# A linear-attention and feed-forward kernel: rows of x and w_in in a new order, a planner that counts TensorE's modes, and new order tables

## The chip, the cores and the metric

The kernel runs on one core of one Trainium2 chip. The metric is device time in microseconds (us) of one execution; lower is better. Engine names in the profile are PE (TensorE's matmuls), PEld (TensorE's loads of stationary operands, which overlap the matmuls), DVE (VectorE), ACT (ScalarE), POOL (GpSimd) and SP (SyncE, which here only issues transfers).

## What is computed

The reference has two parts. The first is a linear attention with a decaying state, for 4 batches of 8 heads, 768 positions and 48 values per head (inputs r, k, v, w and u):

```python
for t in range(S):
    cur = np.einsum('bhd,bhe->bhde', u[None] * kt, vt)
    y[:, :, t] = np.einsum('bhd,bhde->bhe', rt, state + cur)
    state = wt[:, :, :, None] * state + np.einsum('bhd,bhe->bhde', kt, vt)
```

Its output, put together over the heads, is x with 3072 rows of 384 values. The second part is `h = maximum(x @ w_in, 0)` and then `(h * h) @ w_out`, with w_in 384 x 2048 and w_out 2048 x 384, both in 64-bit floats in memory.

## The kernel before

The 768 positions are cut into 6 chunks of 128. An attention unit is one chunk of one batch: `attention(c, b)`. A unit loads w, k and r (two batches at a time, tile st), brings them to a layout with head values on partitions (tile pt: in chunk 0 by TensorE transposes, L443; later by a DVE transpose, L411, and transfers from tile to tile, L421), runs a scan over w on DVE (L455), makes scaled r and k (L466 to L475), and then uses TensorE four times: the scores k by r (L503), transposes of k (L515), the mix of old state and masked scores into y (L528 and L537; in chunk 0 L552 in place of L528), and the update of the state, called dS (L588). The masked scores come from DVE (L507) into tiles that ACT filled with a diagonal (L492).

Heads go in pairs: head 2p at partitions 0 to 47 and head 2p+1 at 64 to 111. The tile xT, the input of the feed-forward part, has three parts of 128 partitions. Pairs 0, 1 and 2 each take one part, at partitions 0-47 and 64-111; the 96 rows of pair 3 are cut into six pieces of 16, which fill partitions 48-63 and 112-127 of the three parts (transfers `send`, L577, from tile x3). The rows of w_in have the same order: `load_w` loads each of 8 column groups of w_in with four transfers, each of which writes 16 or 48 neighbouring partitions of all three parts, and w_out's group with one transfer over all 128 partitions. `split_w` then makes two 32-bit parts from each 64-bit number, on ACT, DVE and POOL (L362 to L383).

The feed-forward part, `ffn`, goes by 16 column blocks f for each chunk: 9 matmuls into hp (L617), then ACT and DVE make two parts of the squared positive values (L622 to L626), then 3 matmuls for each of four batches into ob (L632). In chunk 0 the first 6 blocks, and in chunk 1 all 16, are done for two batches at a time (HALF), so that they can begin when two units are ready.

The order of all this on every engine is not written by hand. Each step is handed to `Plan.add` with an engine, an estimated cost and a rank, and `Plan.order` plays the kernel through: at each point it takes, for each engine, the step that can start first, and among those that can start at the same time the one of lowest rank. The resulting order is what the engines execute. Ranks come from tables in `Ranks`: for unit (c, b) with c of 2 or more the rank of a step is 32(c-1) + 8b - 4 plus an entry of AT; chunk 0 and chunk 1 have bases U0 and C1 and tables AT0 and AT1. The feed-forward steps have the running count x (2 for each full block, 1 for a half one, so 32 for a chunk) plus an entry of OFF, and LAG times the step for ob and os. Where the plan leaves TensorE idle early on, it puts in filler: transposes of the identity into a free PSUM bank (L658), a number that the tuple IDLE sets.

The model of the transfers is in `Plan.order` too: QUEUES has the cost of one issue, RUNS and LANES limit what is outstanding, SLACK is added to each landing.

Of the kernel before, what the change touches and what calls it, by code (L numbers as in the profile page):

```python
# [35 lines left out]
class Plan:  # L36
# [19 lines left out]
    def add(self, engine, cost, rank, fn, r=(), w=(), after=(), runs=128, port=False):  # L56
        s = Step()
        s.engine, s.cost, s.rank, s.fn, s.n, s.runs = engine, cost, rank, fn, len(self.steps), runs
# [18 lines left out]
    def order(self):  # L77
# [4 lines left out]
        free, wait, lanes, wire, sent, out = {}, {}, [], dict.fromkeys(self.QUEUES, 0.0), {}, []  # L82
# [3 lines left out]
        due, idle = {}, 0.0  # L86
# [4 lines left out]
        while len(out) < len(self.steps):  # L91
# [12 lines left out]
            for engine, l in wait.items():  # L104
                unit = "act" if engine == "actq" else engine
                at, pick = None, None
                for s in l:
# [13 lines left out]
                    if pick is None or (t, s.rank) < (at, pick.rank):  # L121
                        at, pick = t, s
# [4 lines left out]
            bank = next((x[1] for p in ("a", "hp") if p in self.pools for x in self.pools[p] if x[0] <= idle), None)  # L127
# [22 lines left out]
            else:  # L150
                free[unit] = at + s.cost
                if s.port:
# [3 lines left out]
            s.fill = 0, None  # L156
            if s.engine == "pe":
                if at < self.IDLE[0] and bank is not None:
                    s.fill = max(0, int((at - max(idle, self.IDLE[1]) - self.IDLE[2]) / self.IDLE[3])), bank
                idle = free["pe"]  # L160
# [22 lines left out]
class Ranks:  # L183
    AT = {'load': -12.5, 'z': -10, 'pt': -10.5, 'rk': -7.0, 'beta': -5.0, 'far': 9.25, 'v': -6.0, 'scan': -2.25, 'ln': 7.0, 'rt': -6, 'kn': 3.25, 'diag': -3.5, 'mt': 5, 'mask': 3.25, 'ktp': 5.25, 'kt': 12.5, 'mix': 4.25, 'x': 1.5, 'x3': -5.0, 'send': 3.0, 'dS': 3.5, 'S': 1.25}
    AT0 = {'load': -13.0, 'turn': -1.5, 'rk': -2, 'beta': 0.2, 'far': 9.25, 'v': -6.75, 'scan': -1.75, 'ln': 5.25, 'rt': 0.25, 'kn': 2, 'diag': 9.5, 'mt': -1.0, 'mask': 3.75, 'ktp': 7.25, 'kt': -1, 'mix': 3, 'x': 7.75, 'x3': -1, 'send': 4.0, 'dS': 7.5, 'S': -4}
    AT1 = {'load': -12.5, 'z': -10, 'pt': -10.5, 'rk': -7.0, 'beta': -5.0, 'far': 9.25, 'v': -6.0, 'scan': -2.25, 'ln': 7.0, 'rt': -6, 'kn': 3.25, 'diag': -3.5, 'mt': 5, 'mask': 3.25, 'ktp': 5.25, 'kt': 12.5, 'mix': 4.25, 'x': 1.5, 'x3': -5.0, 'send': 3.0, 'dS': 3.5, 'S': 1.25}
    U0 = (-16, -15.25, -6.75, -5.5)
    C1 = (5.25, 13, 34.5, 36)
    W0 = (-12.5, -9.5, -1, 0.25, 0.25, 5.5, 5.0, 17)
    WL = (-8.25, -8, -9, -5.5, -1.75, -7, -8.25, -13.5)  # L190
    OFF = {'hp': -1.0, 'g': -6.5, 'ob': 0.75, 'os': -7.5}
# [26 lines left out]
def kernel(  # L218
# [11 lines left out]
    nc = tc.nc  # L230
# [34 lines left out]
    sel = place("sel", [HP, KT, J], F32, placed[f"ro{NG - 2}"])  # L265
    last_y = [place(f"ly{i}", [HP, C], F32, placed[f"ro{NG - 2}"] + 1024 * (i + 1)) for i in range(2)]
# [23 lines left out]
    Ss = [at.tile([HP, NP, J], F32, name=f"S{b}") for b in range(B)]  # L290
# [17 lines left out]
    P.pool("v", [at.tile([128, H * D], F32, name=f"v{i}") for i in range(3)])  # L308
# [15 lines left out]
    for j in range(2):  # L324
        G.affine_select(out=sel[:, :, D:J], in_=sel[:, :, D:J], pattern=[[-(D // KT), KT], [-1, D // KT]],
                        compare_op=ALU.not_equal, fill=1.0, base=-j * J, channel_multiplier=1)
# [15 lines left out]
    def load_w(g, rank):  # L342
        before = first_use(0) if g == NG - 1 else [s for s in P.steps if any(x.pool == "ly" for x in s.slots)] if g == NG - 2 else []

        pairs = w_in32[g, 0:KT * R].rearrange("(k p) x -> p k x", k=KT)
        for j in range(2):
            last = w_in32[g, KT * R + j * D:KT * R + j * D + D].rearrange("(k p) x -> p k x", k=KT)
            for i, (to, n, src) in enumerate(((j * J, D, pairs[j * D:j * D + D]), (j * J + D, J - D, last))):
                P.add("sp", 1.4 if n == D else 0.5, rank, lambda to=to, n=n, src=src: nc.sync.dma_start(out=wi_r[g][to:to + n], in_=src),
                      w=[("wi", g, j, i)], after=before if g == NG - 1 else [], runs=3 * n)  # L350
        P.add("sp", 2.4, rank, lambda: nc.sync.dma_start(out=wo_r[g], in_=w_out32[g]), w=[("wo", g, 0, 0)],
              after=before, runs=256)

    def split_w(g, rank):
        for nm, rt, tt, parts in (("wi", wi_r[g], wi_t[g], [("wi", g, j, i) for j in range(2) for i in range(2)]),
# [33 lines left out]
    def attention(c, b, rank):  # L389
# [40 lines left out]
        vt = Slot("v")  # L430
        P.add("sp", 1.1, rank("v"), lambda: nc.sync.dma_start(out=vt.tile.rearrange("s (h d) -> s h d", d=D),
                                                              in_=v[b, :, ss, :].rearrange("h s d -> s h d")), w=[vt], runs=128 * H)
        if c == 0:
            home = (["o0", "o1", "o2"], ["o3", "hp", "hp"], ["o2", "o3", "a"], ["o2", "o3", "a"])[b]
            ps = {}
            for i, h in zip((0, 2, 1), (home[0], home[2], home[1])):
# [7 lines left out]
                P.add("pe", 0.6, rank("turn"), turn, r=[(st, ui, i)], w=[ps[i]])  # L444
# [74 lines left out]
        yb = Slot("a")  # L519
        ybv = lambda: yb.tile.rearrange("a (p s) -> a p s", p=NP)  # L520

        wide = (J, D)

        def inter():
            for p in range(NP):
# [236 lines left out]
```

## Time and profile before

| | us |
|---|---|
| median of 3 runs | 556.5 |
| lowest and highest | 555.59 and 556.8 |
| the profiled execution, its own time | 557.48 |
| its span, first to last instruction | 555.7 |
| mean granted TensorE clock in it | 0.988 |

| engine | busy us | share of the span |
|---|---|---|
| PE | 539.2 | 97% |
| PEld | 476.3 | 86% |
| DVE | 359.1 | 65% |
| ACT | 287.6 | 52% |
| POOL | 101.8 | 18% |

A share of busy time is a mean over stages with different limits, and a busy TensorE can also be busy with filler, so the stages have to be looked at one by one. In rows of the timeline a matmul's duration overlaps the next one's; the difference of two starts says how much of the engine a group took. A float matmul on 32-bit data stands in the trace as two records.

### The profile page before, as it was taken

The numbers are of one execution on the slowest core, as the hardware profiler recorded it, in microseconds if no ns is written. First come the engines' busy times: TensorE is split into PE (matmuls) and PEld (weight loads), VectorE is DVE, ScalarE is ACT, GpSimd is POOL, SyncE is SP. The second block draws the span as 40 slices with busy tenths as digits, with TensorE's granted clock in tenths as the row PEclk, the third lists the DMA queues.
The fourth block names the chain that finished last, engine by engine and source line by source line (L and its number), as shares of the span: only waits on it lengthen the run. The fifth ranks groups of instructions, "written<-read, shape, count | busy, mean of one in ns | idle before, by whom it ended". The sixth has DMA issues, their size and how long they took to land. (4 is left out here: it accounts for less than half of the span.)

```text
span 555.7 us, 10317 instructions
## 1 busy us (share of the span) xinstructions
PE 539.2 (97%) x3922; PEld 476.3 (86%) x3922; DVE 359.1 (65%) x643; ACT 287.6 (52%) x677; POOL 101.8 (18%) x115
## 2 busy tenths in 40 slices
PE   7898999999999999999999999999999999999995
PEld 6687888889998999888888888888888888999995
DVE  5889889988669595867856657467475343333331
ACT  2785875776745737564644545544563222332222
POOL 4262633541203021030402103002000000000000
PEclk8898999999999999999999999999999999999998
DMA  9999799456373555547460480460430000010001
GB/s 156 202 243 216 131 228 218 75 91 138 82 135 68 111 107 91 110 90 132 86 122 4 84 185 13 83 121 2 85 101 5 10 1 1 15 57 2 0 1 61
DMA packets 206327, 50.88 MB, mean 92 GB/s; under 512 B 196032, under 2 KB 201152, under 8 KB 206272
## 3 DMA queue, kind: packets, MB, share of 16 engines
q1 hardware_dynamic: 205552, 49.17, 44.5%
q10 hardware_dynamic: 720, 0.98, 0.6%
q8 instruction: 33, 0.54, 0.4%
q14 instruction: 22, 0.18, 0.1%
HBM read 31.65 MB, written 4.72 MB: 65 GB/s over the span
## 5 line engine op out<-in xcount | busy, mean ns | idle before, releaser
L632 PE MATMUL ob<-wo,g 128*128 128x384 f32 x1152 | 224.9, 341 | 1.0 <-ACT g L625 1.0
L617 PE MATMUL hp<-x,wi 128*128 128x512 f32 (+1 forms) x1062 | 223.4, 356 | 2.0 <-DVE g L626 2.0
L632 PEld LDWEIGHTS ob<-wo,g 128*128 128x128 f32 x1152 | 200.8, 189 | 8.7 <-ACT g L625 1.2
L617 PEld LDWEIGHTS hp<-x,wi 128*128 128x128 f32 x1062 | 173.8, 188 | 28.6 <-DVE g L626 2.9
L623 DVE SCALAR_TENSOR_TENSOR hp<-hp,t 128x512 f32<-128x512 f32 (+1 forms) x118 | 70.1, 595 | 110.5 <-ACT t L622 110.0
L622 ACT ACTIVATE t<-hp 128x512 f32<-128x512 f32 (+1 forms) x118 | 60.8, 516 | 134.2 <-PE hp L617 108.8
L626 DVE TENSOR_TENSOR g<-hp,g 128x512 fp32r<-128x512 f32 (+1 forms) x118 | 69.0, 585 | 36.9 <-ACT g L625 35.1
L625 ACT CAST g<-hp 128x512 fp32r<-128x512 f32 (+1 forms) x118 | 59.4, 504 | 54.2 <-DVE hp L623 54.1
L492 ACT ACTIVATE m<-ident,beta 128x128 f32<-128x128 f32 x192 | 60.5, 396 | 7.0 <-DVE beta L485 7.0
L482 POOL TENSOR_TENSOR st<-st 128x384 f32<-128x384 f32 x24 | 25.2, 1049 | 66.2 <-DVE st L411 64.7
L507 DVE COPY_PREDICATED m<-caus,a 128x512 f32<-128x512 uint8 x48 | 33.0, 730 | 5.5 <-PE a L503 5.5
L503 PEld LDWEIGHTS a<-pt 48*128 48x128 f32 x384 | 24.2, 189 | 9.2 <-issue 5.1
L503 PE MATMUL a<-pt 48*128 48x128 f32 x384 | 29.2, 287 | 2.3 <-DVE pt L475 2.3
L455 DVE TENSOR_TENSOR_SCAN pt<-pt,zero 112x128 f32<-112x128 f32 x80 | 28.9, 410 | 0.3 <-DMA x<-x 0.3
L570 DVE SCALAR_TENSOR_TENSOR x<-a,x 112x128 fp32r<-112x128 f32 (+2 forms) x44 | 17.9, 431 | 17.1 <-ACT x L569 16.9
L537 PE MATMUL a<-m,v 128*48 128x128 f32 (+1 forms) x384 | 27.6, 285 | 1.0 <-ACT m L492 0.8
L569 ACT ACTIVATE x<-a 112x128 fp32r<-112x128 f32 (+2 forms) x44 | 15.2, 389 | 25.6 <-PE a L537 25.3
L484 POOL TENSOR_TENSOR st<-st,un 128x384 f32<-128x384 f32 x24 | 27.0, 1125 | 1.6
L411 DVE STREAM_TRANSPOSE st<-st 128x1152 f32<-128x1152 f32 x20 | 26.8, 1359 | 0.0
L597 POOL TENSOR_TENSOR S<-S,Ec 112x192 f32<-112x192 f32 x16 | 8.2, 510 | 101.0 <-DVE S L596 101.0
L537 PEld LDWEIGHTS a<-m,v 128*48 128x48 f32 (+1 forms) x384 | 20.9, 132 | 5.9 <-issue 4.2
L462 ACT ACTIVATE m<-pt 112x512 f32<-112x512 f32 x24 | 15.2, 635 | 20.1 <-DVE pt L455 15.7
(76 smaller groups left out, 422.3 us busy)
## 6 DMA issues: line engine op xcount, KB each, us to landing
pt<-st SPq DMA_DIRECT2D x80, 96.0 KB, 2.3
ro<-in_moe_w_out_dram SPq DMA_DIRECT2D x8, 768.0 KB, 9.6
v<-in_v_dram SPq DMA_DIRECT2D x24, 192.0 KB, 3.1
ri<-in_moe_w_in_dram SPq DMA_DIRECT2D x16, 288.0 KB, 9.4
st<-in_w_dram SPq DMA_DIRECT2D x11, 384.0 KB, 4.5
st<-in_k_dram SPq DMA_DIRECT2D x11, 384.0 KB, 5.5
st<-in_r_dram SPq DMA_DIRECT2D x11, 384.0 KB, 5.4
pt<-st SPq DMA_DIRECT2D x80, 48.0 KB, 2.5
```

What stands on the lines that cost most here:

```text
L455: lambda p=p: V.tensor_tensor_scan(out=pt[:, 0, p], data0=src(0)[:, p], data1=zero.broadcast_to([HP, C]), initial=1.0, op0=ALU.mult, op1=A ...
L484: P.add("pool", 1.0, rank("rk"), lambda: G.tensor_tensor(out=rk(), in0=rk(), in1=un.rearrange("s (h d) -> s h d", d=D), op=ALU.mult), w=[( ...
L492: A.activation(mv(j)[:, p], ident, AF.Copy, scale=beta.tile[:, 2 * p + j:2 * p + j + 1])
L503: T.matmul(mts[j].tile.rearrange("s (p t) -> s p t", p=NP)[:, p], pt[js, 2, p], pt[js, 1, p], start=True, stop=True)
L507: lambda j=j: V.copy_predicated(out=mv(j), mask=caus.unsqueeze(1).broadcast_to([128, NP, C]), data=mts[j].tile.rearrange("s (p t) -> s p t ...
L537: T.matmul(ybv()[j * J:j * J + n_, p], vt.tile[:, o:o + n_], mv(j)[:, p], start=(c == 0 and p == KT), stop=True, skip_group_check=True)
L617: T.matmul(hp.tile[:, 0:n], wi[f][:, wl, kt], xT[:, kt, xl, xs], start=(m == 0), stop=(m == 3 * KT - 1))
L622: P.add("act", 0.5 if full else 0.28, rank("g"), lambda: A.activation(t(), h(), AF.Relu), r=[hp], w=[(g, 1)])
L623: P.add("dve", 0.61 if full else 0.33, rank("g"), lambda: V.scalar_tensor_tensor(out=h(), in0=h(), scalar=0.0, in1=t(), op0=ALU.max, op1=A ...
L625: P.add("act", 0.53 if full else 0.31, rank("g"), lambda: A.copy(out=hi(), in_=h()), r=[hp], w=[(g, 0)])
L626: P.add("dve", 0.61 if full else 0.33, rank("g"), lambda: V.tensor_tensor(out=lo(), in0=h(), in1=hi().bitcast(F32), op=ALU.subtract), r=[h ...
L632: T.matmul(obs[b][:, 0:DM], g.tile[0][:, gl, o:o + C], wo[f][:, wl], start=(f == 0 and m == 0), stop=(f == NF - 1 and m == 2))
```

## The change

Rows. The pairs that fill a part of xT are now 0, 2 and 3, at partitions 16 to 111 without a gap (head 2p at 16-63, head 2p+1 at 64-111), and the pair that is cut into pieces is pair 1, at partitions 0-15 and 112-127. For w_in this means pieces of neighbouring rows that span both halves of the partitions: five transfers for a group in place of four, over 112, 112, 96, 16 and 16 partitions. In the attention, the 16 columns that stand beside a head's 48 in a matmul of 64 columns lie ahead of them, not behind; so the tiles of v and S get 16 columns of zeros in front, chunk 0 gets v tiles of its own (64 columns for a head, four of them, in room that weight group 6 takes over later), and the selection matrix `sel` is made by six selects.

Planner. TensorE steps carry a mode: 0 for the whole array, 1 for scores, 3 for the mix and the update. A step whose mode is another than the last one's adds SWITCH = 0.094 us to the time after it, and while TensorE is in another mode than 0, steps that are not in mode 0 have KEEP = 1.0 taken off their rank. The costs of transfers, issues and some matmuls are set anew, and the number of filler transposes too.

Tables. All ranks are new.

```diff
-    QUEUES = {"sp": 0.65, "actq": 0.36}
-    LANES, RUNS, SLACK = 8, 2300, 3.0
-    IDLE = (110.0, 3.2, 0.4, 0.14)
+    QUEUES = {"sp": 0.5, "actq": 0.36}
+    LANES, RUNS, SLACK, START = 8, 2300, 2.0, 2.4
+    SWITCH, KEEP = 0.094, 1.0
+    IDLE = (110.0, 4.0, 0.3, 0.12)
...
-                    if pick is None or (t, s.rank) < (at, pick.rank):
-                        at, pick = t, s
+                    order = s.rank - self.KEEP if engine == "pe" and mode and s.mode else s.rank
+                    if pick is None or (t, order) < (at, first_order):
+                        at, pick, first_order = t, s, order
...
+                if unit == "pe":
+                    if s.mode != mode:
+                        free[unit] += self.SWITCH
+                        mode = s.mode
+                    idle = free[unit]
...
-    AT = {'load': -12.5, 'z': -10, 'pt': -10.5, 'rk': -7.0, 'beta': -5.0, 'far': 9.25, 'v': -6.0, 'scan': -2.25, 'ln': 7.0, 'rt': -6, 'kn': 3.25, 'diag': -3.5, 'mt': 5, 'mask': 3.25, 'ktp': 5.25, 'kt': 12.5, 'mix': 4.25, 'x': 1.5, 'x3': -5.0, 'send': 3.0, 'dS': 3.5, 'S': 1.25}
+    AT = {'load': -105.75, 'z': 279.5, 'pt': 293.75, 'rk': -330.75, 'beta': 21.25, 'far': 18.25, 'v': 60.25, 'scan': 43, 'ln': 19.75, 'rt': 19.5, 'kn': 51, 'diag': -5.25, 'mt': -159, 'mask': 173.5, 'ktp': -201.5, 'kt': 16.25, 'mix': 5.25, 'x': -131, 'x3': -22.5, 'send': 36, 'dS': 23, 'S': 10.5}
...
+    AT1 = {'load': -20.75, 'z': -9.75, 'pt': -57, 'rk': -13, 'beta': 104.5, 'far': 35.25, 'v': -5.75, 'scan': -5.25, 'ln': -68, 'rt': -39.75, 'kn': 2, 'diag': 120.5, 'mt': -311.5, 'mask': -60.25, 'ktp': -46.5, 'kt': -83, 'mix': -111.75, 'x': -6.75, 'x3': -270.75, 'send': -105.75, 'dS': -29.75, 'S': 8.75}
-    C1 = (5.25, 13, 34.5, 36)
-    OFF = {'hp': -1.0, 'g': -6.5, 'ob': 0.75, 'os': -7.5}
+    C1 = (9.25, 16.75, 53.25, 46)
+    OFF = {'hp': 2.75, 'g': -5.75, 'ob': 4, 'os': 64.5}
...
+    PC = J - D
+    TILES, SPLIT = (0, 2, 3), 1
+    SIDE = ((0, 0), (2, 1), (1, 2))
...
+    for t in first_v:
+        V.memset(t.rearrange("s (h x) -> s h x", h=H)[:, :, 0:PC], 0.0)
+    for t in vts:
+        V.memset(t[:, 0:PC], 0.0)
...
-        pairs = w_in32[g, 0:KT * R].rearrange("(k p) x -> p k x", k=KT)
-        for j in range(2):
-            last = w_in32[g, KT * R + j * D:KT * R + j * D + D].rearrange("(k p) x -> p k x", k=KT)
-            for i, (to, n, src) in enumerate(((j * J, D, pairs[j * D:j * D + D]), (j * J + D, J - D, last))):
-                P.add("sp", 1.4 if n == D else 0.5, rank, lambda to=to, n=n, src=src: nc.sync.dma_start(out=wi_r[g][to:to + n], in_=src),
+        raw, rows = wi_r[g], w_in32[g]
+        pieces = ((raw[PC:128, 0], rows[0:128 - PC]), (raw[0:128 - PC, 1], rows[3 * J - PC:4 * J + 2 * PC]), (raw[PC:128 - PC, 2], rows[KT * R:KT * R + R]),
+                  (raw[0:PC, 0:KT:2], rows[3 * D:3 * D + 2 * PC].rearrange("(k p) x -> p k x", k=2)),
+                  (raw[128 - PC:128, 1:KT], rows[R + PC:R + D].rearrange("(k p) x -> p k x", k=2)))
+        for i, (to, src) in enumerate(pieces):
+            n = 2 * PC if i >= KT else to.shape[0]
+            P.add("sp", 0.4 if i >= KT else 0.0059 * n, rank, lambda to=to, src=src: nc.sync.dma_start(out=to, in_=src),
...
-            for p in range(NP):
+            for p in (*TILES, SPLIT):
                 for j in range(2):
-                    T.matmul(ybv()[j * J:j * J + wide[j], p], Ss[b][js, p, 0:wide[j]], pt[js, 1, p],
-                             start=(p == 0), stop=False, skip_group_check=True)
+                    js, n = slice(j * J, j * J + D), ahead(p, j)
+                    T.matmul(ybv()[j * J:j * J + n + D, spot(p)], Ss[b][js, PC + p * D - n:PC + p * D + D], pt[js, 1, p],
+                             start=(spot(p) == 0), stop=False, skip_group_check=True)
```

More of the change, by code (lines that the diff above doesn't have):

```diff
@@ L54, in pool, with add @@
         self.pools[name] = [[0.0, t] for t in tiles]
-    def add(self, engine, cost, rank, fn, r=(), w=(), after=(), runs=128, port=False):
+    def add(self, engine, cost, rank, fn, r=(), w=(), after=(), runs=128, port=False, mode=0):
         s = Step()
+        s.mode, s.fill = mode, (0, None)
         s.engine, s.cost, s.rank, s.fn, s.n, s.runs = engine, cost, rank, fn, len(self.steps), runs
@@ L560, in mix @@
                 inter()
-                part(range(NP))()
-            P.add("pe", 2.0, rank("mix"), mix, r=[vt, *Ms, ("S", b), *RK], w=[yb])
+                part((*TILES, SPLIT))()
+            P.add("pe", 1.94, rank("mix"), mix, r=[vt, *Ms, ("S", b), *RK], w=[yb], mode=3)
             if ui == 0:
```

115 lines of the change are left out of this document (60 added, 55 removed).

## The prediction

> **What bounds the kernel now.** I read the page's engine line first, then busy time by stage, then TensorE's order of work, then the transfers. One execution has this span, and TensorE is busy in nearly all of it:
>
> ```profile
> span 555.7 us, 10317 instructions
> ...
> PE 539.2 (97%) x3922; PEld 476.3 (86%) x3922; DVE 359.1 (65%) x643; ACT 287.6 (52%) x677; POOL 101.8 (18%) x115
> ```
>
> An average over unlike stages, so it is cut into stages. Columns: stretch, its length, busy time of PE, PEld, DVE, ACT, POOL, TensorE's granted clock, DMA share, GB/s.
>
> ```profile
> 0.00:31.20 31.20, 25.76 (x210) 21.22 (x211) 23.09 (x48) 16.91 (x41) 12.13 (x24) 0.89 1.08 182
> 31.20:60.00 28.80, 25.84 (x233) 22.77 (x232) 25.16 (x40) 19.96 (x50) 14.99 (x13) 0.94 1.07 225
> 60.00:94.00 34.00, 32.05 (x222) 29.23 (x221) 29.54 (x52) 26.39 (x59) 13.50 (x8) 1.00 0.91 198
> 94.00:549.50 455.50, 455.50 (x3263) 403.06 (x3262) 281.31 (x505) 223.35 (x527) 61.14 (x72) 1.00 0.34 68
> 549.50:555.70 6.20, 0.03 (x1) 0.00 (x0) 0.00 (x0) 0.96 (x2) 0.00 (x0) 0.73 0.35 126
> ```
>
> From 94 us to 549.5 us TensorE has no idle time at full clock: there only less work on TensorE itself can help. Before 94 us it is short of work. It idles 31.20 - 25.76, 28.80 - 25.84 and 34.00 - 32.05 us, 10.4 us in all, and part of its busy time is the filler of L658, transposes of the identity whose result nobody reads:
>
> ```profile
> L658 PE MATMUL a<-ident 128*128 128x128 f32 x64 | 10.1, 323 | 1.6 <-POOL ident masks.py:199 1.6
> L658 PE MATMUL hp<-ident 128*128 128x128 f32 x58 | 7.2, 276 | 0.0
> ```
>
> So 10.4 + 17.3 = 27.7 us of the first 94 us do nothing for the result. In the same stretches DVE is busy 23.09, 25.16 and 29.54 us and the DMA share is near 1: two other resources are close to full. The last 6.2 us are the output's copies and stores, and no part of the change touches them.
>
> **Switching TensorE between shapes.** The planner gains a cost per change of mode (0: whole array; 1: 48 rows; 3: 64 columns or fewer) and a bonus for staying out of mode 0. What a change costs shows in starts (a listed duration overlaps the next). Undisturbed feed-forward work late in the span:
>
> ```profile
> 509.61 2.27 PE L632 MATMUL ob<-wo,g 128*128 128x384 f32 x12
> 511.71 2.24 PE L617 MATMUL hp<-x,wi 128*128 128x512 f32 x9
> 513.79 1.40 PE L632 MATMUL ob<-wo,g 128*128 128x384 f32 x7
> ```
>
> Twelve matmuls of L632 take 511.71 - 509.61 = 2.10 us, nine of L617 take 2.08 us. Around an attention unit:
>
> ```profile
> 300.65 1.09 PE L537 MATMUL a<-m,v 128*64 128x128 f32 x16
> 301.67 0.60 PE L515 MATMUL a<-ident,pt 112*128 112x112 f32 x4
> 302.04 2.34 PE L617 MATMUL hp<-x,wi 128*128 128x512 f32 x9
> 304.31 0.66 PE L588 MATMUL a<-v,m 128*64 128x48 f32 x16
> 304.91 2.37 PE L632 MATMUL ob<-wo,g 128*128 128x384 f32 x12
> 307.12 2.26 PE L617 MATMUL hp<-x,wi 128*128 128x512 f32 x9
> ```
>
> Here L617 takes 304.31 - 302.04 = 2.27 us before the state update of L588, and L632 takes 307.12 - 304.91 = 2.21 us behind it: 2.27 + 2.21 - 2.08 - 2.10 = 0.30 us over. The first of the two also follows L515's transposes, so I charge 0.10 us to a change and 0.20 us to an excursion out of mode 0 and back. The counts:
>
> ```profile
> L503 PE MATMUL a<-pt 48*128 48x128 f32 x384 | 29.2, 287 | 2.3 <-DVE pt L475 2.3
> L588 PE MATMUL a<-v,m 128*64 128x48 f32 x160 | 13.1, 226 | 0.3 <-ACT m L517 0.2
> ```
>
> At 16 records of L503 and 8 of this form of L588 to a unit there are 24 units with scores and 20 with a state update. Scores, mix and update are each an excursion of their own now, as the row order above shows for the update (L617 lies between).
>
> Do the new tables join them? In rank units, unit (c, b) has its mix at 32(c-1) + 8b - 4 + 5.25 and its update (dS) at 32(c-1) + 8b - 4 + 23. So the update of one unit has 1.75 over the mix of the unit two later, and less the bonus of 1.0 it has 0.75 over. In a chunk of whole feed-forward steps (x rising by 2), hp stands at x + 2.75 and ob at x + 4 + 4. Taking x and the chunk's start as zero, the third unit's mix at 17.25 falls between the hp at 16.75 and the ob at 18; the first unit's update, at 18 with the bonus, ties with that ob, and the list takes the one that became ready first, the update, whose input has been ready for long. So update follows mix directly, for 10 units (chunks 3 and 4, and the last two of chunk 2). For the other ten the ranks leave it open: chunks 0 and 1 have tables of their own, and chunk 2's first two run beside half steps. If only the ten join it is 10 x 0.20 = 2.0 us; if 16 join (chunk 0 aside), 3.2 us. If updates find no free PSUM bank at that moment, none join, and the gain is 0. I take 2.5 us. Nothing hides it: it lies in the stretch without idle time. The matmuls themselves are as many and as long as before (the 16 extra columns move from behind a head's 48 to ahead of them, at the same width of 64; the split pair loses 16).
>
> **w_in's transfers.** Each group of w_in is 768 KB in 384 rows of 2 KB; today's large pieces write partitions 0-47 or 64-111, so one half at a time. w_out's piece of equal size writes all 128. Two stretches in which mostly one of them runs, w_in first:
>
> ```profile
> 56.00:57.30 1.30, 1.30 (x22) 1.09 (x22) 1.30 (x2) 1.15 (x2) 1.22 (x2) 1.00 1.13 197
> 74.00:78.00 4.00, 4.00 (x29) 4.00 (x29) 2.52 (x5) 2.26 (x6) 2.24 (x2) 1.00 0.95 358
> ```
>
> The DMA engines are as busy in both, and move 197 GB/s against 358 GB/s. 786 KB at these rates is 3.99 us and 2.20 us: the bounds for the new layout. Of its 384 rows 320 go in pieces of 96 to 112 partitions, nearest to w_out's row, and 64 in two pieces of 16 partitions, nearest to w_in's own: 320/384 x 2.20 + 64/384 x 3.99 = 2.5 us. So I take 1.5 us saved for each of the 8 groups, from 0 to 1.8.
>
> [...]
>
> What it is worth is set by what waits for it. The queue's issues, in order:
>
> ```profile
> 10.11 2.53 SPq L349 DMA_DIRECT2D ri<-in_moe_w_in_dram  x4
> 12.68 0.43 SPq L351 DMA_DIRECT2D ro<-in_moe_w_out_dram  x1
> 13.15 0.47 SPq L402 DMA_DIRECT2D st<-in_w_dram  x1
> ...
> 26.71 4.46 SPq L349 DMA_DIRECT2D ri<-in_moe_w_in_dram  x4
> ```
>
> The inputs of units 2 and 3 (13.15) stand behind one group, and the third group's w_in (26.71) ends three. With the DMA share at 1.08 and 1.07 they come 1.5 to 4.5 us earlier. That is where TensorE runs dry:
>
> ```profile
> 36.24 3.54 PE L658 MATMUL hp<-ident 128*128 128x128 f32 x31
> 40.76 1.42 PE L632 MATMUL ob<-wo,g 128*128 128x384 f32 x6 [0.97 <-ACT g L625]
> ...
> 45.63 0.49 PE L503 MATMUL a<-pt 48*128 48x128 f32 x2 [1.31 <-DVE pt L475]
> ```
>
> But what releases it there is ACT and DVE, not a transfer. DVE's idle time after 31.2 us is 28.80 - 25.16 + 34.00 - 29.54 = 8.1 us: with DVE's work unchanged the start cannot shrink by more than that past this point. I take the middle of 1.5 and 4.5, 3.0 us, with 0 and 8.1 us as bounds. The new order of the start (chunk 1's last two units later, from 34.5 and 36 to 53.25 and 46) can make it more, by moving their DVE work out of this stretch, and a worse order less, below nothing too (last rival).
>
> **The edits at nothing.** Seven more memsets on DVE, each at most as large as one of S (L330), and four more selects on POOL, six small ones for two:
>
> ```profile
> 6.76 1.37 DVE L455 TENSOR_TENSOR_SCAN pt<-ob,zero 112x128 f32<-112x128 f32 x4 [3.03 <-PE ob L443]
> 8.20 0.19 POOL L471 COPY Ec<-pt 112x4 f32<-112x4 f32 x1 [1.49 <-DVE pt L455]
> ```
>
> DVE idles 3.03 us ahead of its first scan, POOL 1.49 us ahead of its first copy, which covers four selects of up to 0.37 us; that copy itself takes 0.19 us. Without the cover four at 0.19 us would put the first unit back by 0.8 us. One more issue per weight group is 0.43 us on SyncE, like the single one at 12.68, 3.4 us in all, in a queue where the four issues at 26.71 take 4.46 us because earlier transfers still fill it. First-chunk v in tiles of its own takes nothing from the path; w_in's group 6 now waits for their last use, as w_out's does today, and is first needed at x = 24 of the first chunk's 32.
>
> **The sum.** The profiled execution took 557.48 us, 1.8 us over its span and 0.98 us over the median of 556.5. 557.48 - 2.5 (changes of mode) - 3.0 (start) = 551.98, and 0.98 less for the median: 551.0 us.
>
> **Rivals.** First, the start stays bound by DVE, at 25.16 of 28.80 us: earlier transfers wait, and only the modes give something. 556.5 - 2.5 = 554.0 us. For it: the releasers at 40.76 and 45.63; against it: DVE's idle 8.1 us.
>
> Second, the new order takes all of that idle time and 16 updates join: 556.5 - 8.1 - 3.2 = 545.2 us. For it: chunk 1's later units free DVE before 94 us; against it: DVE waits there on chains, not on choices alone.
>
> Third, slower: those two units come too late. Their scans stand at 48 and 40.75 where they stood at 32.25 and 33.75, the first of them behind the feed-forward's g (x - 5.75, which is 42.25 when their half is due at x = 48). DVE's room there, and the unit's two largest groups:
>
> ```profile
> 120.00:140.00 20.00, 20.00 (x144) 18.70 (x141) 15.54 (x34) 14.00 (x34) 5.58 (x5) 1.00 0.58 121
> 140.00:160.00 20.00, 20.00 (x186) 18.60 (x185) 12.42 (x25) 12.88 (x40) 4.52 (x5) 1.00 0.59 117
> ```
>
> ```profile
> L507 DVE COPY_PREDICATED m<-caus,a 128x512 f32<-128x512 uint8 x48 | 33.0, 730 | 5.5 <-PE a L503 5.5
> ...
> L455 DVE TENSOR_TENSOR_SCAN pt<-pt,zero 112x128 f32<-112x128 f32 x80 | 28.9, 410 | 0.3 <-DMA x<-x 0.3
> ```
>
> A unit needs 2 x 0.730 + 4 x 0.410 = 3.1 us for these two and, as an estimate, as much again for its other products, sums and transposes: some 12 us for two units. DVE has 40 - 15.54 - 12.42 = 12.0 us free in these 40 us, so it fits only just. If three quarters of it come after the feed-forward has run dry, TensorE waits 9 us: 551.0 + 9 = 560.0 us. It decides from a wait of 5.5 + 1.1 = 6.6 us on.
>
> Fourth, it doesn't do what it says: updates find no bank, the two small pieces eat what the large ones gain: 556.5 us.
>
> **How the numbers follow.** The forecast has 0.46 (its own range 548.5 to 553), the first rival 0.20, the second 0.12, the third 0.13, the fourth 0.09. A measurement of this kernel tells about 0.2%, 1.1 us, from no change. Faster: 0.46 + 0.20 + 0.12 = 0.78; same 0.09; slower 0.13. The range runs from the second rival to the no-change case, 545.2 to 556.6 us, and leaves out the third and part of the second.
>
> **What would show it.** The row order on TensorE: L588's successor directly behind L537's in chunks 3 and 4, and no rise from 2.08 to 2.27 us beside it. A stretch of w_in alone near 310 GB/s. The first time without idle or filler before 94 us, by some 3 us. It is wrong if TensorE idles after 110 us, above all near 150 to 170 us on x; if fillers and idle time before the bound stage still come to 27 us; or if updates stand alone.

## The result, and the profile after

The changed kernel takes 550.15 us (median of 4 runs, 549.26 to 552.63), the kernel before, beside it on the same chip, 556.65 us (4 runs, 555.59 to 556.97). The ratio is 0.9894 with a 95% interval of 0.9857 to 0.9930: faster, by 4 to 8 us. The forecast was 551.0 us.

The profiled execution of the changed kernel took 549.26 us, the lowest of its four, and that of the kernel before 557.48 us, above its median. The two traces are therefore 8.2 us apart where the medians are 6.5 us apart, and a difference between them of a us or two is not yet a difference between the kernels. The engine line of the changed kernel's page:

```profile
PE 532.6 (97%) x3930; PEld 474.5 (87%) x3930; DVE 357.1 (65%) x650; ACT 287.3 (52%) x677; POOL 102.3 (19%) x119
```

TensorE's share is the same 97%, with 6.6 us less of work. By stage, the columns as in the prediction (stretch, length, PE, PEld, DVE, ACT, POOL, granted clock, DMA share, GB/s):

```profile
0.00:31.20 31.20, 26.39 (x248) 22.28 (x249) 24.30 (x56) 18.11 (x44) 14.85 (x31) 1.00 1.05 201
31.20:60.00 28.80, 26.71 (x269) 23.40 (x264) 25.55 (x44) 22.07 (x56) 15.12 (x9) 1.00 1.01 240
60.00:94.00 34.00, 33.41 (x192) 30.26 (x191) 29.89 (x51) 26.31 (x57) 14.71 (x9) 1.00 0.88 197
94.00:541.00 447.00, 446.05 (x3233) 398.53 (x3231) 277.35 (x501) 219.83 (x523) 57.59 (x71) 1.00 0.34 68
```

The last matmul ends at 541.0 us instead of 549.5. From 94 us on there is still hardly any idle time (0.95 us), so the whole gain shows as a shorter stretch behind 94 us: a part because the start did more of the work, a part because the work itself became shorter.

The first part shows in the feed-forward matmuls that are done by 94 us. A window with the instructions of one line gives it; the columns are stretch, length, PE busy, PEld busy, granted clock, DMA share, GB/s. The two lines (into hp, into ob) of the kernel before:

```profile
0.00:94.00 94.00, 24.46 (x144) 20.40 (x144) 0.95 1.02 201
...
0.00:94.00 94.00, 19.06 (x90) 16.52 (x90) 0.95 1.02 201
```

and of the changed kernel:

```profile
0.00:94.00 94.00, 27.48 (x156) 22.76 (x157) 1.00 0.98 211
...
0.00:94.00 94.00, 21.77 (x108) 18.45 (x108) 1.00 0.98 211
```

24.46 + 19.06 = 43.5 us before, 27.48 + 21.77 = 49.3 us after, 5.7 us more. Of attention the same 304 records lie before 94 us in both, so no other work was put off for it. The remaining 8.5 - 5.7 = 2.8 us of the shorter stretch are in the work behind 94 us; without the 0.95 us of idle time there, that work itself is 3.7 us shorter.

This second part shows in TensorE's order. The timeline of the changed kernel at the same place as in the prediction (start, duration, engine, line, operands, count; L552 and L560 are the mix, L611 the update, L640 and L655 the feed-forward):

```profile
300.22 2.26 PE L640 MATMUL hp<-x,wi 128*128 128x512 f32 x9
302.42 1.08 PE L552 MATMUL a<-pt,S 48*64 48x128 f32 x16
303.43 1.09 PE L560 MATMUL a<-m,v 128*64 128x128 f32 x16
304.35 0.62 PE L611 MATMUL a<-v,m 128*48 128x48 f32 x16
304.90 2.35 PE L655 MATMUL ob<-wo,g 128*128 128x384 f32 x12
307.09 2.24 PE L640 MATMUL hp<-x,wi 128*128 128x512 f32 x9
```

The update stands directly behind the mix; the whole-array L640 that lay between them is gone from there. The two ends of the joined group still cost some 0.1 us each: L640 takes 302.42 - 300.22 = 2.20 us ahead of it and L655 307.09 - 304.90 = 2.19 us behind it, where undisturbed ones take 2.08 and 2.10 us. What is saved is the second excursion. Counted over all of TensorE's instructions in the trace, the changes of mode fell from 132 to 102.

### The profile page after: what moved, and what is told of

Same layout as the page of the kernel before. It is cut to its first block, busy times and chain, and to the rows that moved or that the text cites. A ratio compares the mean times of both kernels' runs of the same rounds, so it can differ in the third digit from the quotient of the medians.

```text
span 547.3 us, 10350 instructions
## 1 busy us (share of the span) xinstructions
PE 532.6 (97%) x3930; PEld 474.5 (87%) x3930; DVE 357.1 (65%) x650; ACT 287.3 (52%) x677; POOL 102.3 (19%) x119
## 5 line engine op out<-in xcount | busy, mean ns | idle before, releaser
L655 PE MATMUL ob<-wo,g 128*128 128x384 f32 x1152 | 226.9, 341 | 0.5 <-ACT g L648 0.5
L640 PE MATMUL hp<-x,wi 128*128 128x512 f32 (+1 forms) x1062 | 222.7, 355 | 1.4 <-DVE g L649 0.9
L655 PEld LDWEIGHTS ob<-wo,g 128*128 128x128 f32 x1152 | 199.3, 188 | 9.2 <-ACT g L648 0.7
L640 PEld LDWEIGHTS hp<-x,wi 128*128 128x128 f32 x1062 | 174.5, 188 | 27.5 <-DVE g L649 2.3
L649 DVE TENSOR_TENSOR g<-hp,g 128x512 fp32r<-128x512 f32 (+1 forms) x118 | 68.9, 585 | 38.1 <-ACT g L648 37.3
L505 POOL TENSOR_TENSOR st<-st 128x384 f32<-128x384 f32 x24 | 26.6, 1108 | 61.7 <-DVE st L432 54.5
L478 DVE TENSOR_TENSOR_SCAN pt<-pt,zero 112x128 f32<-112x128 f32 x80 | 30.3, 426 | 3.0 <-DMA v<-in_v_dram 1.3
L560 PE MATMUL a<-m,v 128*48 128x128 f32 (+1 forms) x384 | 27.2, 279 | 1.0 <-DVE m L530 1.0
L560 PEld LDWEIGHTS a<-m,v 128*48 128x48 f32 (+1 forms) x384 | 20.0, 128 | 6.4 <-issue 4.6
L507 POOL TENSOR_TENSOR st<-st,un 128x384 f32<-128x384 f32 x24 | 25.1, 1047 | 1.6
L404 POOL TENSOR_TENSOR wi<-q,wi 128x768 fp32r<-128x768 f32 x8 | 17.6, 2204 | 38.0 <-ACT wi L403 31.5
L495 DVE TENSOR_TENSOR pt<-pt,m 112x512 f32<-112x512 f32 x24 | 17.4, 728 | 8.9 <-ACT m L486 8.3
```

The lines of the kernel that those rows point to most:

```text
L478: lambda p=p: V.tensor_tensor_scan(out=pt[:, 0, p], data0=src(0)[:, p], data1=zero.broadcast_to([HP, C]), initial=1.0, op0=ALU.mult, op1=A ...
L560: T.matmul(ybv()[to:to + n + D, spot(p)], vt.tile[:, o - n:o + D], mv(j)[:, p], start=(c == 0 and p == SPLIT), stop=True, skip_group_check ...
L640: T.matmul(hp.tile[:, 0:n], wi[f][:, wl, kt], xT[:, kt, xl, xs], start=(m == 0), stop=(m == 3 * KT - 1))
L649: P.add("dve", 0.61 if full else 0.33, rank("g"), lambda: V.tensor_tensor(out=lo(), in0=h(), in1=hi().bitcast(F32), op=ALU.subtract), r=[h ...
L655: T.matmul(obs[b][:, 0:DM], g.tile[0][:, gl, o:o + C], wo[f][:, wl], start=(f == 0 and m == 0), stop=(f == NF - 1 and m == 2))
```

## The experiments

All ratios are to the kernel before, run beside each experiment; 0.001 is 0.56 us. Experiments sent at different times are compared by their ratios.

**The changed kernel again.** No edit.

> The changed kernel once more, as the yardstick for the other three. Both theories: 549 to 551 us, ratio to the kernel before near 0.989. If the granted clock of the first 60 us is 1.00 in the profile again, the clock theory keeps its ground; if it is near 0.91 as before the change and the time is still 550 us, the clock theory falls.

Measured: 0.9902 (0.9882 to 0.9922), 550.47 us, so the result holds. Its trace, of a run of 552.56 us, has 26.77 + 20.05 = 46.8 us of feed-forward work done by 94 us, not 49.3: the start differs by some 2.5 us from one execution to the next.

**The filler of before.**

```diff
-    IDLE = (110.0, 4.0, 0.3, 0.12)
+    IDLE = (110.0, 3.2, 0.4, 0.14)
```

> The changed kernel with the old numbers for filler, IDLE = (110.0, 3.2, 0.4, 0.14): 103 filler transposes in place of 130, nothing else moves in any order. Theory of the prediction (the start gains by earlier transfers): no change, 550 us. Theory of the clock (the start gains since TensorE keeps its full clock, where before the change the granted clock was 0.91 over the first 60 us, 60 x 0.09 = 5.4 us of clock lost): the clock falls again in the first 60 us, and the time rises by 1.5 to 5 us.

Measured: 0.9918 (0.9887 to 0.9949), 551.48 us, with 103 fillers instead of 130. 0.9 us over the unchanged kernel's ratio, with intervals that overlap: not told apart from nothing.

**w_in cut at partition 64, one half after the other.** Each of the three large pieces is cut in two, and the eight pieces of a group go out low half first, then high half, in the five places that the plan has. Rows, tables and plan are the changed kernel's.

```diff
+        low = ((raw[PC:J, 0], rows[0:D]), (raw[0:J, 1], rows[3 * J - PC:4 * J - PC]), (raw[PC:J, 2], rows[KT * R:KT * R + D]), pieces[3])
+        high = ((raw[J:128, 0], rows[D:128 - PC]), (raw[J:128 - PC, 1], rows[4 * J - PC:4 * J + 2 * PC]), (raw[J:128 - PC, 2], rows[KT * R + D:KT * R + R]), pieces[4])
+        halves = (low[0:2], low[2:4], high[0:1], high[1:2], high[2:4])
...
```

> The changed kernel with w_in's bytes cut at partition 64 and sent one half after the other, eight transfers for a group in the five planned places, the order of everything else kept. Theory of the prediction: w_in runs near 197 GB/s again and the start loses what the transfers gave, 3.0 us (1.5 to 4.5): 551.5 to 554.5 us. Theory of the clock: transfers stand off the path, the time rises by less than 1 us.

Measured: 0.9989 (0.9970 to 1.0008), 555.6 us: nearly the whole gain is lost, 0.0087 or 4.8 us, a little more than expected. It is not that one half merely comes first: the first step of `split_w` reads all pieces of a group, so only the last one to land counts. To read how much of that is due to the halves and how much to three more transfers in a group, the same eight pieces were sent in another order.

**The same eight pieces, the halves taking turns.** The edit is against the kernel with the halves one after the other.

```diff
-        halves = (low[0:2], low[2:4], high[0:1], high[1:2], high[2:4])
+        halves = ((low[0], high[0]), (low[1], high[1]), (low[2], high[2]), low[3:4], high[3:4])
```

> A control for w_in_halves: the same eight pieces of w_in for a group, cut at partition 64, but issued low, high, low, high, so that neighbours in the queue write both halves at once. Theory (one half at a time is what is slow): the time comes back to that of the changed kernel, 550 to 552 us. Rival (three more issues for each of 8 groups, 24 x 0.43 us on SyncE, are what cost 5 us): 555 to 556 us as with the halves in order.

Measured: 0.9920 (0.9899 to 0.9942), 551.95 us. So of the 0.0087 that the halves one after another lose, 0.9989 - 0.9920 = 0.0069, 3.8 us, belong to the order low, then high, and 0.0018, 1.0 us with overlapping intervals, to the three pieces more. w_out's issues on the queue of SP stand between w_in's and show how it runs late (first to last issue start is the pair of times behind the durations); halves one after another, then taking turns:

```profile
L379 SPq DMA_DIRECT2D ro<-in_moe_w_out_dram x8: 385/424/1228, 14.3 to 93.5; - x8
```

```profile
L379 SPq DMA_DIRECT2D ro<-in_moe_w_out_dram x8: 385/404/632, 13.9 to 86.7; - x8
```

The last group is issued at 93.5 us in the first, 86.7 us in the second (81.6 us in the changed kernel, 85.2 us in the kernel before). The feed-forward work done by 94 us follows. Halves one after another (into hp, into ob), then taking turns:

```profile
0.00:94.00 94.00, 25.16 (x144) 20.87 (x144) 0.96 0.91 190
...
0.00:94.00 94.00, 17.92 (x84) 15.08 (x85) 0.96 0.91 190
```

```profile
0.00:94.00 94.00, 26.85 (x154) 22.18 (x155) 1.00 0.94 208
...
0.00:94.00 94.00, 21.66 (x108) 18.45 (x108) 1.00 0.94 208
```

43.1 us against 48.5 us, with the same bytes, the same pieces and the same plan. The rate itself shows in a stretch that holds hardly anything but w_in's packets (2 KB each, where w_out's are 3 KB), halves one after another first, then taking turns:

```profile
85.30:88.30 3.00, 3.00 (x11) 2.70 (x10) 2.08 (x4) 2.44 (x6) 2.08 (x1) 0.62 1.09 211
```

```profile
79.60:82.10 2.50, 2.50 (x14) 2.12 (x13) 2.26 (x4) 2.17 (x5) 2.44 (x2) 1.00 1.05 265
```

At nearly the same DMA share 211 GB/s become 265 GB/s.

**The updates alone again.** One entry of the table, so that the update no longer ties with the step behind the mix.

```diff
-    AT = {..., 'dS': 23, ...}
+    AT = {..., 'dS': 19, ...}
```

> The changed kernel with the rank of dS in AT at 19 in place of 23, so that the updates of chunks 2 to 4 no longer follow a mix: 120 changes of mode on TensorE in place of 102, the order of the first 150 us kept. At 0.10 us for a change the time rises by 1.8 us, whatever the start does, since TensorE has no idle time there. Rival: a change of mode costs nothing of its own (the rises seen beside it are how matmul ends are modelled): no rise.

Measured: 0.9942 (0.9921 to 0.9962), 552.65 us, and 120 changes of mode. 0.0040 over the unchanged kernel, 2.2 us for 18 changes: 0.12 us a change. The two intervals just touch, so the 2.2 us may be some 0.6 to 3.8 us. The start of its trace does not explain them: 26.76 + 20.56 = 47.3 us of feed-forward work are done by 94 us, between the 46.8 and the 49.3 us of the changed kernel's two traces. The order has become that of before, with L640 between:

```profile
299.67 1.56 PE L640 MATMUL hp<-x,wi 128*128 128x512 f32 x6
301.16 0.67 PE L611 MATMUL a<-v,m 128*64 128x48 f32 x16
301.75 2.37 PE L655 MATMUL ob<-wo,g 128*128 128x384 f32 x12
```

**The rows alone.** The new rows, pieces and v tiles, with the planner and all tables of before.

```diff
...
-    SWITCH, KEEP = 0.094, 1.0
...
-    OFF = {'hp': 2.75, 'g': -5.75, 'ob': 4, 'os': 64.5}
+    OFF = {'hp': -1.0, 'g': -6.5, 'ob': 0.75, 'os': -7.5}
...
-            P.add("sp", 0.4 if i >= KT else 0.0059 * n, rank, lambda to=to, src=src: nc.sync.dma_start(out=to, in_=src),
+            P.add("sp", 0.3 if i >= KT else 0.01 * n, rank, lambda to=to, src=src: nc.sync.dma_start(out=to, in_=src),
```

> The new rows, w_in pieces, v tiles and matmul widths, but the planner and the tables of before (w_in's five pieces counted at 3.8 us together as before, no modes). Theory of the prediction (the transfers alone give 3.0 us, 1.5 to 4.5): 552 to 555 us. Rival (the order made for slow transfers cannot use fast ones, the gain needs the new tables): 556 to 557 us.

Measured: 1.0471 (1.0444 to 1.0499), 583.0 us, far slower than either expectation. The stages and two rows of its timeline (in brackets the idle time before, and what ended it):

```profile
150.00:200.00 50.00, 40.50 (x342) 35.28 (x341) 36.56 (x71) 28.15 (x77) 10.29 (x14) 0.83 0.45 91
200.00:250.00 50.00, 46.46 (x419) 42.59 (x415) 35.62 (x78) 26.28 (x74) 8.93 (x12) 0.90 0.55 105
```

```profile
191.28 2.50 PE L520 MATMUL a<-pt 48*128 48x128 f32 x16 [2.62 <-DVE pt L492]
...
203.83 2.29 PE L634 MATMUL hp<-x,wi 128*128 128x256 f32 x9 [3.54 <-DMA x<-x]
```

TensorE is out of work in a stretch where the kernel before has no idle time and the changed one next to none: it waits for the scores' operands of a late unit, and the feed-forward waits for that unit's part of x. 9.5 + 3.5 = 13 us are idle, and a part of the rest is slower, in stretches with a granted clock of 0.83 and 0.90: the scores' 16 records take 2.50 us at 191.28 us and 1.16 us at 166.00 us, nine of L634 2.29 us at 203.83 us and 1.24 us at 147.96 us. The loss is not in the start: 24.48 + 19.18 = 43.7 us of feed-forward work are done by 94 us, as in the kernel before, although w_in alone runs at 256 and 259 GB/s in two stretches of this trace. The new rows under the planner and the tables of before are worth less than nothing. Two further kernels look at which part of the tables matters.

**All tables of before, in the changed kernel.** Rows, planner, modes and filler stay new; only the class of ranks is that of before.

```diff
...
-    C1 = (9.25, 16.75, 53.25, 46)
...
-    OFF = {'hp': 2.75, 'g': -5.75, 'ob': 4, 'os': 64.5}
...
+    C1 = (5.25, 13, 34.5, 36)
...
+    OFF = {'hp': -1.0, 'g': -6.5, 'ob': 0.75, 'os': -7.5}
```

> The changed kernel and planner with all rank tables of before: 130 changes of mode on TensorE in place of 102, 152 filler transposes. If the tables were worth only the joined updates: 550.5 + 28 x 0.10 = 553.3 us, with no idle time on TensorE after 110 us. If, as with the planner of before, the old ranks put chunk 1's last two units too late in the new rows: TensorE idles between 150 and 250 us and the time is 560 to 585 us.

Measured: 1.0124 (1.0094 to 1.0154), 564.35 us, so under the new rows and planner the tables carry 0.0222, 12.4 us. 28 of the changes of mode are back (130), at 0.12 us some 3.4 us. Of feed-forward work 24.27 + 18.04 = 42.3 us are done by 94 us, 4.5 to 7.0 us less than in the changed kernel's two traces. Together that is most of the 12.4 us. A part of the start:

```profile
31.20:60.00 28.80, 24.99 (x230) 21.35 (x226) 28.11 (x41) 21.40 (x56) 12.64 (x10) 0.94 0.98 233
```

DVE is busy 28.11 of 28.80 us there, and TensorE is idle for 3.8 us. The time lies where the second expectation put it, but its reason does not hold: there is no long idle time at 150 to 250 us as with the rows alone. The two kernels have the same tables and the same rows and differ in the planner, its cost numbers and its filler, so those are worth 1.0471 - 1.0124 = 0.0347, 19.3 us, here; which part of them keeps chunk 1's last units in time was not tried. The reverse, the new planner and tables with the rows of before, was not run either.

**Chunk 1's tables of before, in the changed kernel.** AT1 and C1 alone.

```diff
...
-    C1 = (9.25, 16.75, 53.25, 46)
+    C1 = (5.25, 13, 34.5, 36)
```

> The changed kernel with chunk 1's table and bases (AT1, C1) of before, all else new: 108 changes of mode in place of 102, 158 filler transposes. If putting chunk 1's last two units later freed DVE for the start, as the prediction's second rival has it: the stage before 94 us loses 1 to 3 us and the time is 552 to 554 us. If chunk 1's place does not matter: 550.5 + 0.6 = 551.1 us.

Measured: 1.0074 (1.0053 to 1.0095), 562.27 us: with all else new, 0.0172, 9.6 us, hang on when chunk 1 is worked at, far more than either expectation. It has 108 changes of mode, so few of the 9.6 us are due to those. One stage, and one row of TensorE's timeline:

```profile
60.00:94.00 34.00, 26.33 (x157) 23.95 (x156) 26.78 (x43) 22.15 (x52) 12.42 (x9) 0.90 0.87 185
```

```profile
87.02 4.00 PE L640 MATMUL hp<-x,wi 128*128 128x512 f32 x9 [6.29 <-DVE g L649]
```

TensorE is idle for 7.7 of 34 us, 6.29 of them in one wait for g, which DVE makes, and works slowly behind it (4.00 us for nine matmuls that take 2.1). Only 23.46 + 14.78 = 38.2 us of feed-forward work are done by 94 us, 8.6 to 11 us less than in the changed kernel's two traces. DVE is not short of time there: it is busy 26.78 of the 34 us, less than the changed kernel's 29.89. What stands in its queue does it, and its timeline shows what:

```profile
80.29 1.37 DVE L478 TENSOR_TENSOR_SCAN pt<-pt,zero 112x128 f32<-112x128 f32 x4 [2.28 <-DMA pt<-st]
...
82.43 4.20 DVE L489 TENSOR_TENSOR pt<-pt 112x508 f32<-112x508 f32 x1
```

A unit of chunk 1 has its four scans (L478) and the product behind them (L489) ahead of the feed-forward's g in DVE's order. The scans wait 2.28 us for a transfer, the product takes 4.20 us, and only then, at 86.55 us, comes the g that TensorE waits for. The queue of SP is another order too: chunk 1's transfers from tile to tile (L442) hold it for 16.78 us from 61.37 us on, in the changed kernel for 7.37 us from 60.03 us on, and w_out's last group is issued at 90.57 us in place of 81.6 us. How the 9.6 us divide between the two queues was not measured.

**No filler, and more filler.** The line that defines the filler taken out; and, in another kernel, 208 of them instead of 130.

```diff
-    P.filler = lambda bank: T.transpose(out=bank[:, 0:128], in_=ident, identity=ident)
```

> The changed kernel without any filler transposes, the order of everything else kept. If filler is what holds TensorE's clock in the start, the granted clock of the first 60 us falls from 0.97 to 1.00 to 0.85 or less, and the time rises by 3 to 8 us; if attention's own matmuls hold it, nothing changes, 550 to 551 us.

```diff
-    IDLE = (110.0, 4.0, 0.3, 0.12)
+    IDLE = (110.0, 3.0, 0.1, 0.10)
```

> The changed kernel with IDLE = (110.0, 3.0, 0.1, 0.10): 208 filler transposes in place of 130. One profile of the changed kernel had full clock all through the start and took 549.3 us, another fell to 0.94 between 31 and 60 us and took 552.6 us. If more filler keeps the clock, the median goes to 549 us with less spread; if the filler now delays real work, the median rises by 1 to 3 us.

Measured: 0.9947 (0.9928 to 0.9967), 554.71 us without, 2.5 us lost, a little under the expected 3 to 8 us; 0.9935 (0.9915 to 0.9955), 553.02 us with more, 1.8 us lost. The filler is needed, and its amount is near what serves. Without it the first scores take 1.8 times as long (first the kernel without filler, then the changed kernel):

```profile
17.54 2.08 PE L526 MATMUL a<-pt 48*128 48x128 f32 x16 [4.67 <-DVE pt L498]
...
38.09 0.38 PE L640 MATMUL hp<-x,wi 128*128 128x256 f32 x1 [1.70 <-ACT x L591]
```

```profile
17.07 1.16 PE L526 MATMUL a<-pt 48*128 48x128 f32 x16 [0.55 <-DVE pt L498]
...
34.71 0.38 PE L640 MATMUL hp<-x,wi 128*128 128x256 f32 x1 [0.26 <-ACT x L591]
```

16 records take 2.08 us instead of 1.16, and the first feed-forward block begins at 38.1 us instead of 34.7.

**Is the new filler worth something by itself?** The kernel before with the new tuple.

```diff
-    IDLE = (110.0, 3.2, 0.4, 0.14)
+    IDLE = (110.0, 4.0, 0.3, 0.12)
```

> The kernel before with the new numbers for filler, 149 transposes in place of 122, no other order changed. If the clock lost in its start (granted 0.91 over the first 60 us) is what the new numbers mend: 553 to 555.5 us, with a granted clock near 1.00 there. If not: 556 to 557 us.

Measured: 0.9989 (0.9970 to 1.0007), 557.06 us: nothing. The mean granted clock of the first 94 us rose from 0.95 to 0.98, and the feed-forward work done in them stayed at 24.46 + 19.03 = 43.5 us. So a better granted clock in the start gave nothing by itself here, and the changed kernel's gain is not shown to come from it.

**Are the transfers worth something by themselves?** The kernel before, with its own rows, tables and plan, and w_in in eight pieces with the halves taking turns, in the four places that its plan has.

```diff
+        large = [[(raw[j * J:j * J + D, q], rows[q * R + j * D:q * R + j * D + D]) for j in range(2)] for q in range(KT)]
...
+        sent = (large[0] + large[1][0:1], small[0:1], large[1][1:2] + large[2], small[1:2])
...
```

> The kernel before, its rows and its whole order kept, with w_in's group sent as eight pieces that alternate between the two halves of the partitions, in the four planned places. Theory (one half at a time is slow, and the start waits for it): the difference seen between the two cuttings of the changed kernel, 555.6 - 551.95 = 3.65 us, comes here too, less up to 1.5 us for more pieces: 552.5 to 554.5 us. Rival (fast transfers are worth something only in an order made for them): 556 to 557 us.

Measured: 0.9976 (0.9954 to 0.9998), 555.89 us: 1.3 us, between the two expectations, with an interval from 0.1 to 2.6 us. w_in alone runs at 226 and 230 GB/s in two stretches of its trace, against 182 to 205 GB/s in the kernel before, and 24.44 + 19.71 = 44.2 us of feed-forward work are done by 94 us, 0.6 us more than before. Under the new tables, low then high against taking turns is 3.8 us and 5.4 us of such work. The two pairs are not quite alike: here the eight pieces replace four, and four more issues a group may eat some of the gain (three more went with 1.0 us above). With these intervals it is likely, but not shown, that the old order makes less of the same transfers.

## Why the prediction was right, point by point

**The whole.** 551.0 us was forecast and 550.15 us measured, in the own range of the likeliest case. Its two terms come out in size; the start's is what is left of the whole once the modes are taken off. That rows, planner and tables have each a small worth of their own, as a sum of two terms suggests, does not hold: rows and transfers without the planner and the tables cost 26 us, and the tables alone are worth 12.4 us under the new rows and planner.

**The changes of mode** were forecast at 2.5 us. 30 fewer changes, at 0.12 us from the updates set apart, are 3.6 us; at the 0.10 us that was read from the trace, 3.0 us. The term was a little small because the joins were more: the trace shows 15 updates directly behind a mix. All eight of chunks 3 and 4 are among them, as the ranks gave it, three of chunk 2's four (the third in order of time, at 219.11 us, still stands alone, though the prediction had counted the last two), and all four of chunk 0, which it had left aside. None of chunk 1's joined.

**w_in's transfers** were forecast at 2.5 us a group, near 310 GB/s. That was too good. In the changed kernel, three stretches that hold hardly anything but w_in's packets:

```profile
44.50:47.00 2.50, 2.50 (x24) 2.33 (x21) 2.33 (x5) 2.25 (x4) 0.36 (x2) 1.00 0.88 257
50.20:52.70 2.50, 2.50 (x23) 2.38 (x21) 2.50 (x5) 0.85 (x2) 0.93 (x1) 1.00 1.04 271
68.60:71.60 3.00, 2.67 (x20) 2.40 (x19) 2.40 (x5) 3.00 (x8) 1.51 (x1) 1.00 0.88 259
```

786 KB at 257 to 271 GB/s are 2.9 to 3.1 us, and not the 2.5 us of the estimate by rows: about 1.0 us saved for a group, not 1.5 us. Either w_out's 358 GB/s was no near row for pieces of 96 to 112 partitions, or the two small pieces cost more than their share of rows; no run tells which.

**The start** was forecast at 3.0 us. What the medians leave beside the modes is 6.5 - 3.6 to 6.5 - 3.0, 2.9 to 3.5 us, and by the second comparison (550.47 against 556.40, 5.9 us) 2.3 to 2.9 us; the second trace has 46.8 - 43.5 = 3.3 us more of feed-forward work by 94 us. The size fits, and the halves one after another lose 3.8 us against taking turns, as much as the whole term. But the fit is in part luck: with 1.0 us a group the prediction's own step, one to three groups, gives 1.0 to 3.0 us with its middle at 2.0 us. The step also treated the term as the worth of the transfers, whatever the order. With the planner and tables of before, the new rows and pieces bring 43.7 us of feed-forward work by 94 us where 43.5 us were, and the transfers taking turns give the kernel before 1.3 us. The start's gain needs w_in's rate, which the halves show; that the order adds to it is what these runs point to.

**The first rival** (the start stays bound by DVE, 554.0 us) did not happen: 3.3 to 5.7 us more of feed-forward work are done by 94 us, with DVE busy 25.55 of 28.80 us, little more than the 25.16 us before. With the old tables in it DVE is busy 28.11 us there; that DVE is what holds TensorE then was not shown, since the longest waits of that start are for ACT's g (2.7 us), DVE's g (2.0 us) and a transfer (2.0 us).

**The second rival** (all of DVE's idle time is taken) did not happen. DVE's idle time from 31.2 to 94 us is 28.80 - 25.55 + 34.00 - 29.89 = 7.4 us, against 8.1 before. Chunk 1's place is worth much all the same, 9.6 us with all else new, but not in the way that was argued: it does not free DVE's time. What the trace shows is that it takes a unit that waits for a transfer out of the way of the feed-forward's g in DVE's queue.

**The third rival** (chunk 1's last units too late) did not happen here: 0.95 us of idle time after 94 us. Its mechanism is real and was part of the largest loss of all, in the rows alone, where TensorE is idle for 13 us at 150 to 250 us. That kernel has chunk 1's old, earlier ranks, so the later ranks that the prediction blamed are not what makes the units late; the old tables under the new planner don't do it either. The planner and its cost numbers decide it, together with the rows, and the prediction gave the planner no price beyond the modes.

**The fourth rival** is excluded by the interval.

**The edits at nothing** cost nothing that shows. In the changed kernel's first 10 us:

```profile
6.59 0.92 POOL L340 TENSOR_SCALAR_AFFINE_SELECT sel<-sel 112x16 f32<-112x16 f32 x6
7.01 1.37 DVE L478 TENSOR_TENSOR_SCAN pt<-ob,zero 112x128 f32<-112x128 f32 x4 [2.81 <-PE ob L466]
...
8.44 0.19 POOL L494 COPY Ec<-pt 112x4 f32<-112x4 f32 x1 [0.79 <-DVE pt L478]
```

Six selects take 0.92 us and end at 7.51 us, and the copy still waits 0.79 us for DVE. DVE still idles 2.81 us ahead of its first scan, which starts 0.25 us later than before.

**Signs that were wrong.** The stretch of w_in alone near 310 GB/s was not there, as said above. The prediction also called itself wrong if filler and idle time before the bound stage still came to 27 us. They do: the two groups of filler before 94 us are

```profile
L681 PE MATMUL a<-ident 128*128 128x128 f32 x97 | 15.0, 303 | 1.6 <-POOL ident masks.py:199 1.6
L681 PE MATMUL hp<-ident 128*128 128x128 f32 x33 | 4.5, 276 | 0.0
```

15.0 + 4.5 = 19.5 us, and TensorE's idle time is 4.81 + 2.09 + 0.59 = 7.5 us, together 27.0 us where 27.7 us were before. The kernel is faster nonetheless, with 5.7 us more of feed-forward work in the same time. A part of the room came from the attention's 304 records, which take 29.6 us before and 26.8 us after, though they are the same. The transposes of the inputs take 6.0 + 2.2 + 1.3 = 9.5 us of it before and 5.2 + 1.3 + 1.3 = 7.8 us after. The scores, before and after:

```profile
L503 PE MATMUL a<-pt 48*128 48x128 f32 x64 | 6.0, 300 | 2.3 <-DVE pt L475 2.3
```

```profile
L526 PE MATMUL a<-pt 48*128 48x128 f32 x64 | 5.1, 286 | 0.8 <-DVE pt L498 0.8
```

The attention gives 2.8 us in all, idle time and filler 0.7, and the rest lies in how far the records overlap. The work done by a time was the measure to name.

## What to carry to other kernels

A planner and its tables belong to the layout and the transfers they were made for: the new rows under the old planner and tables cost 26 us here, under the new ones the kernel is 6 us faster, so a layout can't be judged under an order made for another. Worth trying elsewhere are transfers into the two halves of the partitions at the same time, and steps of one mode directly behind each other. Here w_in ran at 211 GB/s with its pieces cut at partition 64 and one half sent after the other, at 265 GB/s with the halves taking turns, and at 257 to 271 GB/s in pieces of which the large ones span both. Updates put directly behind a mix, 18 changes of mode fewer, were worth 2.2 us, 0.12 us a change, with an interval of some 0.6 to 3.8 us. To see whether a start became better, count the work that is done by a given time, not the idle time, and compare several executions.

## What the runs showed that was not expected

**Pieces that take turns between the halves run nearly like pieces that span both.** The prediction looked for the gain in pieces that span both halves. Here eight pieces, each within one half, are 3.8 us faster when low and high take turns in the queue (0.9920 against 0.9989), with w_in at 265 GB/s against 211 GB/s, and within 1.0 us of five pieces that span both. That was measured with many pieces queued one behind another; two transfers alone were not tried.

**The granted clock said nothing of the first matmuls.** The window of the kernel without filler:

```profile
0.00:31.20 31.20, 19.07 (x115) 14.49 (x116) 21.86 (x49) 16.27 (x39) 12.50 (x28) 1.00 1.12 199
```

It shows 1.00, while the scores at 17.54 us in it take 2.08 us, 1.8 times what they take behind filler. Here the durations of known groups tell the speed, not that column. Up to 17.07 us the changed kernel's TensorE runs nothing but transposes, filler and inputs, and the scores behind them take 1.16 us, as they do at 37.52 us behind feed-forward work.

**A DVE instruction at six times its median, beside two GpSimd instructions.** While L489 takes its 4.20 us in the kernel with chunk 1's old tables, POOL's timeline has two long instructions, and the row of L489 over all its executions there (lowest, median and highest ns) shows how unlike the others it is:

```profile
82.52 1.80 POOL L404 TENSOR_TENSOR wi<-q,wi 128x768 fp32r<-128x768 f32 x1
...
84.29 1.79 POOL L404 TENSOR_TENSOR wo<-q,wo 128x768 fp32r<-128x768 f32 x1
```

```profile
L489 DVE TENSOR_TENSOR pt<-pt x20: 660/677/4200, 82.4 to 408.9; 112x508 f32<-112x508 f32 x20
```

L489 takes 0.677 us in the median of its 20 and 4.20 us here, about the sum of its own time and the two on POOL (0.68 + 1.80 + 1.79 = 4.27 us), with the g for which TensorE waits behind it. That the two on POOL held it was not shown: L489's row starts 0.09 us ahead of theirs, and in the changed kernel L489 at 79.31 us takes 0.68 us although a row of L404 on POOL starts at 79.41 us, before it ends. How much of the 9.6 us this one meeting costs was not measured by itself.
